# Output product by one level of Strassen: seven block products for eight, block sums on GpSimd

## The chip, the cores and the metric

One Trainium2 chip; the program runs on one of its cores. A core has five engines with queues of their own: TensorE (PE in the profile, its weight loads PEld), VectorE (DVE), ScalarE (ACT), GpSimd (POOL) and SyncE (SP), which here only starts DMAs. The engines run in parallel and meet at semaphores; each takes its own instructions in order. TensorE reads SBUF and writes PSUM; DVE and ACT read and write both; GpSimd reads and writes SBUF alone. The metric is the device time of one run in microseconds (us), the median of several.

## The reference

Two stages. Attention through a small memory, for 8 batches of 8 heads, 576 tokens, head width 64 and 32 memory slots; then a bilinear feed-forward over the 4608 tokens.

```python
a = softmax(phi, over tokens)                    # 576 x 32 per head
k_m, v_m = a.T @ k, a.T @ v                      # 32 x 64 each
x = softmax(q @ k_m.T / 8) @ v_m                 # 576 x 64 per head, 8 heads side by side: 512
h = (x @ w1) * (x @ w2)                          # 512 -> 1024, elementwise product
out = (h @ w3) @ w_out                           # 1024 -> 1024 -> 512
```

All inputs and the output are float32; the weights come in as float64.

## The kernel before, in words

Two products are folded ahead of the tokens. W = w3 w_out (1024 x 512) is built once on chip from converted weights ("C" steps convert a tile of float64 to float32 on DVE and ACT, "W" steps are its matmuls, "K" steps take it out of PSUM). For each batch M = v_m w1 and v_m w2 (per head, 256 memory rows against 2 x 1024 columns) is made in four quarters of 256 columns of h, so that x w1 and x w2 become products of the attention weights with M.

To get near float32 from the fast float32r matmul, each operand is split into a rounded high part and the rest (`split`, lines 114 to 116: ACT casts, another engine subtracts), and a product is three matmuls: high by high, high by low, low by high.

A batch passes through two stages on TensorE:

- The A stage: 16 units "A" (`ab_unit`), one for each of 8 row tiles of 128 columns of h and each half of 288 tokens. A unit is 12 matmuls of 128x128 weights against 288 columns: 6 into a PSUM bank "a" (x w1) and 6 into a bank "b" (x w2). ACT copies a to `a_sb` (line 458), DVE multiplies b by it into `gr` (line 460), and `gr`, which is G of `out = G W`, is split into `gh` and `gl` (line 463).
- The output stage: row tiles of 128 tokens. A tile is four steps "O" (`out_part`) of 6 matmuls: weights are 128 tokens of G, moving are the 512 columns of W. 24 matmuls add up in one bank "o"; ACT copies it to `osb`, and a DMA stores it. 576 is four and a half tiles, so odd batches do five tiles and even ones four; 36 in all.

Between these units stand the attention steps of the next batch and the one after, by name: `top` (maximum mx of phi on DVE, line 162), `exp` (ACT, line 168), `turn0` and `turn4` (transposes of phi on TensorE, line 184 and 188, copied by ACT), `mem` (memories, line 199), `blocks` (transposes, line 224, and four DVE copies to km and vm), `sc` (scores), `se`, `sn`, `pr` (softmax over the memories and the split into `ah` and `al`), and the M steps (line 298, then split into `mh` and `ml`).

PSUM has 8 banks: two each of "a", "b" and "o", and one pair "x". The pair x serves the transposes, `blocks`, half of the scores and some M steps; whoever comes next into x waits until the engine that reads it has finished. In the kernel before, M steps written "Mp" use banks a and b instead, "M" uses x, and all four for the next batch stand in the output stage.

The order on TensorE and on SyncE is the order of the program, which the strings START, FIRST, SECOND and STEADY write out by hand: FIRST is batch 0, SECOND batch 1, STEADY the rest; a name with "+" belongs to the batch after next. The order on DVE, ACT and GpSimd is set by a scheduler that moves instructions by a model of their times. `fetch` and `load` issue DMAs; a load goes out when its tile is free.

Of the kernel before, what the change touches and what calls it, by code (L numbers as in the profile page):

```python
# [35 lines left out]
mem+ sc0 sc1p Mp O kv3 se0 O se1 O q2 sn0 O pr0 O sn1 O pr1 M Mp Mp O O phi3 O O blocks+ O O O O O O Oo Oo Oo Oo  # L36
# [4 lines left out]
def memory_attention__then__bilinear_ffn_kernel(  # L41
# [22 lines left out]
    P = 128  # L64
# [7 lines left out]
    DO = w_out.shape[1] // 2  # L72
    HALF = S // 2
# [17 lines left out]
    half = NF // 2  # L91

    def w_half(r):

        return [const.tile([P, half, DO], F32R, name=f"W{x}{r}") if r == 0 else
                const.tile([P, half, DO], F32R, name=f"W{x}{r}", tag=f"wo{i}") for i, x in enumerate("hl")]

    Wh, Wl = [list(x) for x in zip(w_half(0), (None, None))]
# [56 lines left out]
    def attention(b):  # L155
# [129 lines left out]

    m_tags = (2, 3, 4, 0, 5, 6, 7, 1)

    def memory_weights(b):
# [3 lines left out]
        def step(q, banks):  # L292
# [12 lines left out]
            mh = const.tile([P, NT, 2, FQ], F32R, name=f"mh{q}", tag=f"m{m_tags[2 * q]}")  # L305
            ml = const.tile([P, NT, 2, FQ], F32R, name=f"ml{q}", tag=f"m{m_tags[2 * q + 1]}")
# [22 lines left out]
    raws, w3s = {}, {}  # L329
    free_m = [1, 2, 3, 4, 0, 5, 6, 7, 1]  # L330
    wos = [const.tile([P, half, DO], F32, name=f"wo{i}", tag=f"wo{i}") for i in range(2)]
# [18 lines left out]
    def convert(i):  # L350
# [3 lines left out]
        if kind == "w12":  # L354
            y = w12_sb[at[0]][:, at[1]]
        elif kind == "wo":
            y = wos[at // half][:, at % half : at % half + n]
        else:
            y = const.tile([P, n, CW // 2], F32, name="w3", tag=f"m{free_m.pop(0)}")
            for j in range(n):  # L360
                w3s[int(kind[2]), at + j] = y[:, j]
        if i < FIRST_LATE:
            u = init.tile([P, CW], I32, name="u", bufs=2)
        elif i % 2:
            u = att.tile([P, 5 * NT * P], I32, name="ua", tag="a")
        else:
            u = att.tile([P, 2, S], F32R, name="al", tag="al", bufs=2).rearrange("p t s -> p (t s)").bitcast(I32)
# [18 lines left out]
    def product(r, k):  # L386
# [3 lines left out]
        x = w3s.pop((r, k))  # L390
        for i in range(4):
            nc.tensor.matmul(  # L392
                pw[r][i],
                lhsT=x[:, i * P : (i + 1) * P],
                rhs=wos[k // half][:, k % half],
                start=k == 0,
                stop=k == NF - 1,
            )

    def keep(r, i):  # L400
        if r == 1 and Wh[1] is None:
            Wh[1], Wl[1] = w_half(1)
        split(Wh[r][:, i], Wl[r][:, i], pw[r][i])
# [8 lines left out]
    with tc.tile_pool(name="init", bufs=1) as init:  # L412
# [4 lines left out]
        for what in START:  # L417
# [4 lines left out]
            elif what[0] == "K":  # L422
                keep(int(what[1]), int(what[2]))
# [155 lines left out]
```

## Time and profile before

| | us |
|---|---|
| median of 3 runs | 551.91 (551.74 to 552.37) |
| span of the profiled execution | 548.7 |
| median beyond that span | 3.2 |
| TensorE busy | 531.0 |
| DVE, ACT, GpSimd busy | 306.7, 248.9, 14.0 |

The profile is of one execution. A row of a timeline gives start, duration, engine, line, operation, output and inputs, and in brackets the idle time before it with what ended it. A row of groups ends with busy time, mean of one in ns, and the engine's idle time before them. Matmuls are pipelined: the duration of one is longer than the distance to the next, so rates are read from starts.

### The profile page before, as it was taken

The numbers are of one execution on the slowest core, as the hardware profiler recorded it, in microseconds if no ns is written. First come the engines' busy times: TensorE is split into PE (matmuls) and PEld (weight loads), VectorE is DVE, ScalarE is ACT, GpSimd is POOL, SyncE is SP. The second block draws the span as 40 slices with busy tenths as digits, with TensorE's granted clock in tenths as the row PEclk, the third lists the DMA queues.
The fourth block names the chain that finished last, engine by engine and source line by source line (L and its number), as shares of the span: only waits on it lengthen the run. The fifth ranks groups of instructions, "written<-read, shape, count | busy, mean of one in ns | idle before, by whom it ended". The sixth has DMA issues, their size and how long they took to land.

```text
span 548.7 us, 9743 instructions
## 1 busy us (share of the span) xinstructions
PE 531.0 (97%) x4024; PEld 427.4 (78%) x4024; DVE 306.7 (56%) x584; ACT 248.9 (45%) x494; POOL 14.0 (3%) x22
## 2 busy tenths in 40 slices
PE   4799999999999999999999999999999999999997
PEld 1344357976998689968996899869986899689985
DVE  4877996357367715593458425673567045915400
ACT  5886966524454325452544335443544044514310
POOL 0000004400000000000000000000000000000000
PEclk9999999999999999999999999999999999999999
DMA  8999827036334510072008210351022100010011
GB/s 300 408 361 391 295 77 272 31 113 229 118 139 171 171 40 20 2 278 82 20 1 280 81 39 1 149 174 57 1 59 69 39 20 2 20 44 15 1 38 57
DMA packets 24987, 64.05 MB, mean 117 GB/s; under 512 B 1776, under 2 KB 2032, under 8 KB 24944
## 3 DMA queue, kind: packets, MB, share of 16 engines
q1 hardware_dynamic: 24944, 63.45, 32.6%
q8 instruction: 31, 0.51, 0.4%
q14 instruction: 12, 0.10, 0.1%
HBM read 54.00 MB, written 9.44 MB: 116 GB/s over the span
## 4 chain that ended last, share of the span: by engine, by line
PE 89%; DVE 6%; DMA 2%; issue 1%; ACT 1%; SPq 0%; DVEq 0%; ACTq 0%
PE o L473 37%; PE b L449 18%; PE a L449 18%; PE a L298 2%; PE a L392 2%; PE b L392 2%; DMA raw<-in_w3T 2%; PE o L199 2%; PE x L298 2%; DVE w L382 2%; PE x L184 1%; PE b L298 1%; PE x L199 1%; PE x L239 1%; DVE w L381 1%
## 5 line engine op out<-in xcount | busy, mean ns | idle before, releaser
L473 PE MATMUL o<-Wh,gh 128*128 128x512 f32 x288 | 115.4, 401 | 0.0
L473 PE MATMUL o<-Wl,gh 128*128 128x512 f32 x288 | 112.8, 391 | 0.0
L473 PE MATMUL o<-Wh,gl 128*128 128x512 f32 x288 | 112.5, 391 | 0.0
L460 DVE TENSOR_TENSOR gr<-b,a_sb 128x288 f32<-128x288 f32 x128 | 58.6, 458 | 94.0 <-PE b L449 87.0
L115 ACT CAST gh<-gr 128x288 fp32r<-128x288 f32 x128 | 55.4, 433 | 100.8 <-DVE gr L460 100.5
L116 DVE TENSOR_TENSOR gl<-gr,gh 128x288 fp32r<-128x288 f32 x112 | 51.2, 458 | 55.5 <-ACT gh L115 55.3
L449 PE MATMUL b<-ah,mh 128*128 128x288 f32 x256 | 76.0, 297 | 1.7 <-DVE gr L460 1.2
L449 PE MATMUL a<-ah,mh 128*128 128x288 f32 x256 | 77.3, 302 | 0.0
L449 PE MATMUL a<-al,mh 128*128 128x288 f32 x256 | 75.6, 295 | 0.1
L449 PE MATMUL b<-al,mh 128*128 128x288 f32 x256 | 75.5, 295 | 0.0
L449 PE MATMUL a<-ah,ml 128*128 128x288 f32 x256 | 75.3, 294 | 0.0
L449 PE MATMUL b<-ah,ml 128*128 128x288 f32 x256 | 75.3, 294 | 0.0
L473 PEld LDWEIGHTS o<-Wh,gh 128*128 128x128 f32 x288 | 54.1, 188 | 22.6 <-issue 11.9
L491 ACT COPY osb<-o 128x512 f32<-128x512 f32 x31 | 18.1, 585 | 100.5 <-PE o L473 87.7
L473 PEld LDWEIGHTS o<-Wl,gh 128*128 128x128 f32 x288 | 54.1, 188 | 12.4
L473 PEld LDWEIGHTS o<-Wh,gl 128*128 128x128 f32 x288 | 54.1, 188 | 10.9
L458 ACT COPY a_sb<-a 128x288 f32<-128x288 f32 x128 | 50.2, 394 | 3.3 <-PE a L449 3.3
L449 PEld LDWEIGHTS a<-ah,mh 128*128 128x128 f32 x256 | 48.0, 187 | 3.1 <-issue 1.0
L449 PEld LDWEIGHTS b<-ah,mh 128*128 128x128 f32 x256 | 48.0, 187 | 2.4 <-DVE gr L460 1.6
L449 PEld LDWEIGHTS a<-al,mh 128*128 128x128 f32 x256 | 48.1, 188 | 0.7 <-DVE al L116 0.3
L449 PEld LDWEIGHTS b<-ah,ml 128*128 128x128 f32 x256 | 48.2, 188 | 0.0
L449 PEld LDWEIGHTS a<-ah,ml 128*128 128x128 f32 x256 | 48.2, 188 | 0.0
(98 smaller groups left out, 663.1 us busy)
## 6 DMA issues: line engine op xcount, KB each, us to landing
kv<-in_kv SPq DMA_DIRECT2D x16, 1024.0 KB, 7.2
q<-in_qT SPq DMA_DIRECT2D x8, 1152.0 KB, 10.7
out<-osb SPq DMA_DIRECT2D x31, 256.0 KB, 2.0
raw<-in_w3T SPq DMA_DIRECT2D x7, 1024.0 KB, 11.9
ph<-in_phiT SPq DMA_DIRECT2D x8, 576.0 KB, 3.9
raw<-in_w SPq DMA_DIRECT2D x4, 1024.0 KB, 16.4
raw<-in_w_out SPq DMA_DIRECT2D x3, 1024.0 KB, 10.5
kv<-in_w SPq DMA_DIRECT2D x3, 1024.0 KB, 14.3
```

The source lines that it names most:

```text
L115: nc.scalar.copy(out=hi, in_=src)
L116: engine.tensor_tensor(out=lo, in0=src, in1=hi.bitcast(F32), op=ALU.subtract)
L184: nc.tensor.transpose(ps[:, c, t], v["ph"][:, t, at : at + P], ident)
L199: nc.tensor.matmul(ps[t][h * M : (h + 1) * M, : 2 * D], lhsT=v["a"][:, i, t, h * M : (h + 1) * M], rhs=kvt[i][:, (4 * t + h) * 2 * D : (4 ...
L298: nc.tensor.matmul(ps[t][g * M : (g + 1) * M], lhsT=vm[b % 2][d, g], rhs=w12_sb[q][d, :, g], start=True, stop=True,)
L382: nc.vector.tensor_tensor(out=y, in0=y, in1=u, op=ALU.add)
L392: nc.tensor.matmul(pw[r][i], lhsT=x[:, i * P : (i + 1) * P], rhs=wos[k // half][:, k % half], start=k == 0, stop=k == NF - 1,)
L449: nc.tensor.matmul(p, lhsT=x[:, t, w, fc : fc + P], rhs=y[:, n, t * HALF : (t + 1) * HALF], start=i == 0, stop=i == len(todo) - 1,)
L458: nc.scalar.copy(out=a_sb, in_=ps[0])
L460: nc.vector.tensor_tensor(out=gr, in0=ps[1], in1=a_sb, op=ALU.mult)
L473: nc.tensor.matmul(v["p"], lhsT=x[f][:, at : at + P], rhs=y[f // half][:, f % half], start=f == 0 and k == 0, stop=f == NF - 1 and k == 2,)
L491: nc.scalar.copy(out=osb, in_=v["p"])
```

## The change

G and W are each cut into 2 x 2 blocks, and `out` is computed with one level of Strassen's method (the variant with 4 sums on either side and shared sums on the output): seven products of blocks for eight. With tokens cut into halves n (288 tokens) and the inner dimension into alternating tiles k, G has blocks `r00, r01, r10, r11` (tile `raw`), one for each half and parity of the tile.

- The operands change places: weights are now blocks of W (128 columns at a time), moving are 288 tokens. The output is stored transposed, 512 x 4608, and turned on the host.
- `weight_sums` forms four differences of W's blocks on GpSimd, once for each half of W's rows; `weight_split` splits the seven block operands into `Th`, `Tl` (ACT casts, GpSimd subtracts for the first half, DVE for the second). `keep` is now a copy alone.
- `ab_unit` writes the product to `raw` (line 486); `add` forms four sums of G's blocks on GpSimd, in place (line 461); `operand` splits a block sum for one product into a slot `s0` to `s3`, subtracting on DVE, and for products 5 and 3 on GpSimd.
- `out_part` is one product j and one half t of 128 output columns: 12 matmuls of 288 columns. The order is 1, 2, 6, 7, 4, 5, 3. Products 1, 6, 7 and 4 add up in banks "o", with a copy of the bank to `ev` after 1, 6 and 7 (line 529); 2, 5 and 3 go to banks a and b, and DVE adds `ev` on the way out (line 541).
- The M tiles get two buffers by parity of the quarter. One M step for the next batch stays in the output stage, and three ("m") go into the batch's own A stage. All use pair x; "Mp" is gone.
- Scratch for the conversions moves to other tiles, `ah` and `al` have one buffer instead of two, and the scratch for software DMAs shrinks to make room.

```diff
 STEADY = """
-A top+ A exp+ A norm+ A A turn0+ A A turn4+ A A A A A A A A A
-mem+ sc0 sc1p Mp O kv3 se0 O se1 O q2 sn0 O pr0 O sn1 O pr1 M Mp Mp O O phi3 O O blocks+ O O O O O O Oo Oo Oo Oo
+A m A top+ A exp+ A A m norm+ A A turn0+ A A m A turn4+ A A A A A A
+mem+ sc0 sc1p O kv3 se0 O se1 O q2 sn0 O pr0 O sn1 O pr1 O M O phi3 O O blocks+ O O O O
...
-            mh = const.tile([P, NT, 2, FQ], F32R, name=f"mh{q}", tag=f"m{m_tags[2 * q]}")
-            ml = const.tile([P, NT, 2, FQ], F32R, name=f"ml{q}", tag=f"m{m_tags[2 * q + 1]}")
+            mh = const.tile([P, NT, 2, FQ], F32R, name=f"mh{q}", tag=f"mh{q % 2}")
+            ml = const.tile([P, NT, 2, FQ], F32R, name=f"ml{q}", tag=f"ml{q % 2}")
...
+    def weight_sums(r):
+        t = late.tile([P, 3, 2, DC], F32, name="sums", tag="ev")
+        b11, b12, b21, b22 = [block(r, k, j) for k in range(2) for j in range(2)]
+        sub = lambda out, x, y: nc.gpsimd.tensor_tensor(out=out, in0=x, in1=y, op=ALU.subtract)
+        sub(t[:, 2], b22, b12)
+        sub(b12, b12, b11)
+        sub(t[:, 1], b22, b12)
+        sub(t[:, 0], b21, t[:, 1])
+        sums[r] = {1: b11, 2: b21, 3: b22, 4: t[:, 0], 5: b12, 6: t[:, 1], 7: t[:, 2]}
...
+        split(Th[j][:, at], Tl[j][:, at], sums[r][j], nc.vector if r else nc.gpsimd)
...
+    HOME = {1: 0, 2: 1, 6: 2, 4: 3, 7: 0, 5: 1, 3: 2}
+
+    def operand(j, i, n=1):
+        if i == 0:
+            s = HOME[j]
+            slots[j] = (big if s < 2 else late).tile([P, 2, NP, TH], F32R, name=f"s{s}", tag=f"s{s}")
+        x = {1: raw[0][0], 2: raw[0][1], 4: raw[1][1], 6: raw[1][1], 7: raw[1][0], 5: raw[0][0], 3: raw[0][1]}[j]
+        h, l = slots[j][:, 0, i : i + n], slots[j][:, 1, i : i + n]
+        split(h, l, x[:, i : i + n], nc.gpsimd if j in (5, 3) else nc.vector)
...
-        nc.vector.tensor_tensor(out=gr, in0=ps[1], in1=a_sb, op=ALU.mult)
-        split(gh[f][:, at : at + HALF], gl[f][:, at : at + HALF], gr, nc.vector if b else nc.gpsimd)
+        i, k = divmod(f, 2)
+        nc.vector.tensor_tensor(out=raw[n][k][:, i], in0=ps[1], in1=a_sb, op=ALU.mult)
+        if (n, k) == (0, 1) and i % 2:
+            operand(1, i - 1, 2)
+            operand(2, i - 1, 2)
+        elif (n, k) == (1, 0):
+            add(a21, a11, a21, ALU.subtract)
+        elif (n, k) == (1, 1):
+            operand(4, i)
+            add(a22, a22, a21, ALU.subtract)
+            if i % 2:
+                operand(6, i - 1, 2)
+                j = slice(i - 1, i + 1)
+                add(raw[0][0][:, j], raw[0][0][:, j], raw[1][1][:, j], ALU.add)
+                add(raw[0][1][:, j], raw[0][1][:, j], raw[1][1][:, j], ALU.subtract)
+
+    ORDER = [(j, t) for j in (1, 2, 6, 7, 4, 5, 3) for t in range(2)]
...
-            for k, (x, y) in enumerate(((gh, Wh), (gl, Wh), (gh, Wl))):
+        for i in range(NP):
+            for k, (w, g) in enumerate(((Th, 0), (Th, 1), (Tl, 0))):
                 nc.tensor.matmul(
-                    v["p"],
-                    lhsT=x[f][:, at : at + P],
-                    rhs=y[f // half][:, f % half],
+                    p,
+                    lhsT=w[j][:, i, c],
+                    rhs=x[:, g, i],
...
+        if t == 1 and j in (1, 2, 6):
+            for i in range(0, NP, 2):
+                operand({1: 7, 2: 5, 6: 3}[j], i, 2)
...
+        if j in (1, 6, 7):
+            nc.scalar.copy(out=ev[:, (1, 6, 7).index(j), t], in_=p)
+            return
...
+        if j == 4:
+            nc.scalar.copy(out=osb[:, t], in_=p)
+        else:
+            nc.vector.tensor_tensor(out=osb[:, t], in0=p, in1=ev[:, {2: 0, 5: 2, 3: 1}[j], t], op=ALU.add)
```

Three places show how the queues change. The first is ACT in the A stage of batch 3, between the copy of turn0 (x to a, 1024 wide) and that of turn4 (x to a, 128 wide). Before:

```order
L185 COPY a_3300<-x_3341 128x1024
L458 COPY a_sb_3365<-a_3351 128x288
L115 CAST gh2_502<-gr_3367 128x288
L458 COPY a_sb_3385<-a_3371 128x288
L189 COPY a_3300<-x_3391 128x128
```

After:

```order
L181 COPY a_2904<-x_2946 128x1024
L484 COPY a_sb_2970<-a_2956 128x288
L111 CAST s3_2868<-r11_506 128x288
L484 COPY a_sb_2995<-a_2981 128x288
L111 CAST s2_2976<-r11_506 128x576
L111 CAST mh3_3007<-x_2998 128x1024
L484 COPY a_sb_3025<-a_3011 128x288
L185 COPY a_2904<-x_3028 128x128
```

Between the two users of x there now stands a third, the batch's last M step (mh3 from x), and one A unit (one a_sb) between it and turn4.

The second is DVE in the A stage of batch 1 around the fifth unit: `gr` and `r00` are the units' products, mx the maximum of phi for batch 3, km and vm the copies of `blocks`. Before:

```order
L116 TENSOR_TENSOR gl1_509<-gr_1307,gh1_501 128x288
L162 TENSOR_REDUCE mx_1471<-ph_1311 128x2
L227 TENSOR_SCALAR km0_77<-x_1384 64x128
L228 COPY vm0_79<-x_1384 64x128
L227 TENSOR_SCALAR km0_77<-x_1384 64x128
L228 COPY vm0_79<-x_1384 64x128
L173 TENSOR_SCALAR sm_1493<-sm_1493 128x2
L460 TENSOR_TENSOR gr_1373<-b_1364,a_sb_1371 128x288
```

After:

```order
L112 TENSOR_TENSOR s3_1389<-r11_506,s3_1389 128x288
L158 TENSOR_REDUCE mx_1549<-ph_1393 128x2
L169 TENSOR_SCALAR sm_1581<-sm_1581 128x2
L170 RECIPROCAL sm_1581<-sm_1581 128x2
L486 TENSOR_TENSOR r00_503<-b_1446,a_sb_1453 128x288
L112 TENSOR_TENSOR s0_1500<-r00_503,s0_1500 128x576
L112 TENSOR_TENSOR ml2_1466<-x_1456,mh2_1465 128x1024
L223 TENSOR_SCALAR km0_77<-x_1476 64x128
```

The copies of `blocks` now come after the fifth unit's product, its split and an M quarter (ml2) that sits in x too; `blocks` takes x right after that M step, with no unit between.

The third is DVE at the end of the product stage of batch 3, after the change: al ends the attention of batch 4, mx belongs to batch 5, and osb are the output additions of product 5 (banks a and b).

```order
L112 TENSOR_TENSOR al_3311<-at_3309,ah_3310 128x576
L112 TENSOR_TENSOR ml0_3377<-x_3367,mh0_3376 128x1024
L158 TENSOR_REDUCE mx_3535<-ph_3393 128x2
L223 TENSOR_SCALAR km1_78<-x_3423 64x128
L224 COPY vm1_80<-x_3423 64x128
L223 TENSOR_SCALAR km1_78<-x_3423 64x128
L224 COPY vm1_80<-x_3423 64x128
L541 TENSOR_TENSOR osb_3443<-a_3430,ev_3231 128x288
```

Before, nothing that TensorE waits for stood behind mx here; now the addition that frees product 5's bank does.

More of the change, by code (lines that the diff above doesn't have):

```diff
@@ L72, in memory_attention__then__bilinear_ffn_kernel @@
     DO = w_out.shape[1] // 2
+    TH = S // 2
     HALF = S // 2
@@ L90, in memory_attention__then__bilinear_ffn_kernel @@
     w12_sb = [const.tile([P, 2, NG, FQ], F32, name=f"w12_{q}") for q in range(NQ)]
[L91 to L98, printed above, removed]
+    NP = NF // 2
+    DC = DO // 2
+    late = ctx.enter_context(tc.tile_pool(name="late", bufs=1))
     def psum(pool, name):
@@ L328, in memory_attention__then__bilinear_ffn_kernel @@
     BUFS = 5
-    raws, w3s = {}, {}
-    free_m = [1, 2, 3, 4, 0, 5, 6, 7, 1]
-    wos = [const.tile([P, half, DO], F32, name=f"wo{i}", tag=f"wo{i}") for i in range(2)]
+    raws, parts_of = {}, {}
+    free_wt = iter(range(14))
     init = None
@@ L389, in product, with block, weight_split @@
             pw[r] = [psum(*x) for x in (tags * 2, ((ps_o, "o"),) * 2 + tags)[r]]
-        x = w3s.pop((r, k))
+        x = parts_of.pop((f"w3{r}", k))
+        y = parts_of["wo", k] if r == 0 else parts_of.pop(("wo", k))
         for i in range(4):
[L392 to L398, printed above, removed]
-    def keep(r, i):
-        if r == 1 and Wh[1] is None:
-            Wh[1], Wl[1] = w_half(1)
-        split(Wh[r][:, i], Wl[r][:, i], pw[r][i])
+            nc.tensor.matmul(pw[r][i], lhsT=x[:, i * P : (i + 1) * P], rhs=y, start=k == 0, stop=k == NF - 1)
+    W, sums, Th, Tl = {}, {}, {}, {}
+    def keep(r, i):
+        if r not in W:
+            W[r] = late.tile([P, NP, DO], F32, name=f"W{r}", tag=f"s{2 + r}")
+        nc.scalar.copy(out=W[r][:, i], in_=pw[r][i])
+    def block(r, k, j):
+        return W[r].rearrange("p (i k) (j c) -> p i k j c", k=2, j=2)[:, :, k, j]
+    def weight_sums(r):
[7 more added lines that the diff above has]
+        sums[r] = {1: b11, 2: b21, 3: b22, 4: t[:, 0], 5: b12, 6: t[:, 1], 7: t[:, 2]}
+    def weight_split(j, r):
+        if r == 0:
+            Th[j], Tl[j] = [const.tile([P, NP, DC], F32R, name=f"T{x}{j}", tag=f"wt{2 * j - 2 + i}") for i, x in enumerate("hl")]
+        at = slice(2 * r, 2 * r + 2)
+        split(Th[j][:, at], Tl[j][:, at], sums[r][j], nc.vector if r else nc.gpsimd)
     todo = iter(range(len(tasks)))
@@ L423, in memory_attention__then__bilinear_ffn_kernel @@
                 keep(int(what[1]), int(what[2]))
+            elif what[0] == "T":
+                weight_sums(int(what[1]))
             elif what == "N":
@@ L499, in memory_attention__then__bilinear_ffn_kernel @@
     for b in range(B):
         v = {}
-        ab = iter([(n, f) for f in range(NF) for n in range(2)])
-        if b == 0:
-            ab = iter([(n, 2 * q + f) for q in range(NQ) for n in range(2) for f in range(2)])
-        parts = iter([(i, part) for i in range((S + b % 2 * REST) // P) for part in range(4)])
+        ab = iter([(n, 2 * i + k) for i in range(NP) for n in range(2) for k in range(2)])
+        parts = iter(ORDER)
+        m_now = m0 if b == 0 else m1
         if b + 1 < B:
@@ L511, in memory_attention__then__bilinear_ffn_kernel @@
                 out_part(b, *next(parts), v)
-            elif what == "Oo":
-                if b % 2:
-                    out_part(b, *next(parts), v)
+            elif what == "m":
+                m_now.pop(0)()
             elif what == "C":
```

99 lines of the change are left out of this document (52 added, 47 removed).

## The prediction

> **What bounds the kernel now.** I read the page's first and fourth parts first: which engine fills the span, and which work the chain that ended last is made of.
>
> ```profile
> span 548.7 us, 9743 instructions
> PE 531.0 (97%) x4024; PEld 427.4 (78%) x4024; DVE 306.7 (56%) x584; ACT 248.9 (45%) x494; POOL 14.0 (3%) x22
> PE 89%; DVE 6%; DMA 2%; issue 1%; ACT 1%; SPq 0%; DVEq 0%; ACTq 0%
> ```
>
> TensorE is the bound: 97% busy, 89% of the chain. DVE and ACT have slack on the average and GpSimd is nearly empty. So columns removed from TensorE come off the time one for one, and so does every new gap on TensorE. The median of the runs, 551.9 us, is 3.2 above this execution's span of 548.7; I make the sum on the span and carry the 3.2 along.
>
> Next the timeline of TensorE in a steady batch, for the pitch of back-to-back matmuls: start of one to start of the next.
>
> ```profile
> 224.75 0.29 PE L449 MATMUL a<-ah,mh 128*128 128x288 f32 x1
> 230.62 0.29 PE L449 MATMUL b<-ah,ml 128*128 128x288 f32 x1
> 235.28 0.39 PE L473 MATMUL o<-Wh,gl 128*128 128x512 f32 x1
> 243.07 0.39 PE L473 MATMUL o<-Wl,gh 128*128 128x512 f32 x1
> ```
>
> Between the first pair lie 44 steps: 5.87/44 = 133.4 ns for 288 columns. Between the second lie 34: 7.79/34 = 229.1 ns for 512. One unit "A" (12 matmuls) is thus 1.60 us.
>
> **The gain.** Before, the output stage has 36 row tiles of 24 matmuls: 864 x 0.2291 = 197.9 us. After, each of 8 batches has 7 products x 2 halves x 12 = 168 matmuls of 288 columns, 1344 in all. Their form (128x128 fp32r weights, 288 moving columns, a weight load each) is exactly the A unit's, so its pitch is the price, loads included: 1344 x 0.1334 = 179.3. That is 18.6 less: 9.4% for an eighth of the columns, because the short matmul is dearer per column. All else on TensorE (A units, four M steps a batch, attention, the weight product) keeps its count.
>
> **What DVE, ACT and GpSimd get, and what hides it.**
>
> ```profile
> L460 DVE TENSOR_TENSOR gr<-b,a_sb 128x288 f32<-128x288 f32 x128 | 58.6, 458 | 94.0 <-PE b L449 87.0 <-PE x L188 3.7 <-ACT gh L115 1.6
> L458 ACT COPY a_sb<-a 128x288 f32<-128x288 f32 x128 | 50.2, 394 | 3.3 <-PE a L449 3.3
> L115 ACT CAST gh<-gr 128x288 fp32r<-128x288 f32 x128 | 55.4, 433 | 100.8 <-DVE gr L460 100.5
> L115 ACT CAST ah<-at 128x576 fp32r<-128x576 f32 x16 | 10.7, 673 | 13.0 <-DVE at L274 13.0
> L116 DVE TENSOR_TENSOR al<-at,ah 128x576 fp32r<-128x576 f32 x16 | 11.5, 753 | 0.6
> L116 POOL TENSOR_TENSOR gl<-gr,gh 128x288 fp32r<-128x288 f32 x16 | 13.3, 834 | 96.5 <-ACT gh L115 96.5
> ```
>
> A batch's splits become 12 casts of 576 at 673 ns and 4 of 288 at 433: 9.8 us of ACT for 6.9 before. On DVE 8 subtractions at 753 and 4 at 458 (7.9 for 7.3) and 6 output adds near 458 (2.7). GpSimd gets 8 operations of 288 (834 ns) and 8 of 576. The last have no row: bounds are 0.83 (all fixed cost) and 1.67 (all per element); I take 1.5, nearer the second since the work is per element. That is 19 us of GpSimd in a batch of some 57. DVE and ACT gain under 4 us each per batch at 56% and 45% use; all this lies beside TensorE, and costs only where a TensorE instruction comes to wait. Walking the new queues with these durations, the operands are in time: the last one made from the final A unit (sum on GpSimd, cast, subtraction) is ready some 3 us after it, and the two products ahead of it take 6.4. Handing bank o from product to product needs a 394 ns copy within a 1.6 us half product. Output DMAs are 4 a batch for 4 or 5, off the path; the tail keeps one evacuation and one store.
>
> **Where TensorE comes to wait: pair x.** M now goes through pair x only, three of its four steps inside the A stage, where the transposes of phi use x too. What an M step through x costs until x is free, in batch 0:
>
> ```profile
> 95.80 1.09 PE L298 MATMUL x<-w,vm 64*32 64x512 f32 x16
> 96.82 0.40 PE L449 MATMUL a<-ah,mh 128*128 128x288 f32 x1
> 96.99 1.02 ACT L115 CAST mh<-x 128x1024 fp32r<-128x1024 f32 x1
> 98.05 1.23 DVE L116 TENSOR_TENSOR ml<-x,mh 128x1024 fp32r<-128x1024 f32 x1 [1.58 <-ACT mh L115]
> ```
>
> M ends at 96.82, x is free at 99.28: 2.46 us. In batches 2 to 5 one A unit stands between the fourth M step and turn4, in batch 1 one between the second and turn0. One unit covers 1.60, so TensorE stands 0.86 each time: 5 x 0.86 = **4.3 us**. Behind the waiting transpose all of TensorE waits. Without the unit as cover it would be 2.46.
>
> In batch 1 `blocks` follows its M step with no unit between: 2.46 at least. DVE's new order makes it longer: the maximum mx for batch 3 stands ahead of the fifth unit's product, and waits for a transfer issued only when turn4 has read phi.
>
> ```profile
> 144.89 0.39 SPq L123 DMA_DIRECT2D ph<-in_phiT  x1
> 148.81 1.35 DVE L162 TENSOR_REDUCE mx<-ph 128x2 f32<-128x1152 f32 x1 [0.85 <-DMA ph<-in_phiT]
> 86.82 0.78 ACT L168 ACTIVATE ph<-ph,mx 128x576 f32<-128x576 f32 x1 [0.57 <-DVE mx L162]
> 88.26 0.19 ACT L168 ACTIVATION_READ_ACCUMULATOR ph<-ph,mx 128x1 f32 x1
> 230.84 1.96 PE L199 MATMUL o<-kv,a 128*32 128x128 f32 x64
> 232.97 0.69 PE L239 MATMUL x<-q,km 64*32 64x288 f32 x16
> ```
>
> From issue to mx 3.92, mx 1.35, the two exponentials 1.63 (86.82 to 88.45). Counted from turn4's end: mx ends 5.3, exponentials 7.0, a_sb 7.4, the product 7.9, its cast 8.6, mh 9.6, ml and x free 10.9. TensorE gets there at 1.60 + 2.13 (memories, 230.84 to 232.97) + 1.60 + 1.02 = 6.35. Stall **4.5 us**; bounds 2.46 (mx not in the way) and 6.
>
> **The same mx behind the products.** In the product stage mx for the batch after next stands ahead of the output add of product 5, whose bank product 3 needs. In batch 0 the scores come three halves into the products. The chain from scores to the last al took 12.4 us in the quoted steady batch:
>
> ```profile
> 243.92 1.43 DVE L116 TENSOR_TENSOR al<-at,ah 128x576 fp32r<-128x576 f32 x2
> ```
>
> (232.97 to 245.35). Scores at 7.2 after the first product begins, al at 19 to 20.7 (the new rows interleave), phi in 3.9 later, mx and the add by 24.7 to 26.4; product 3 wants the bank at 23.6. Stall 1.1 to 2.8; I take **1.5**. In batches 1 to 5 the scores start first, the add is done at about 22.5 and the bank is wanted at 23.6: hidden by 1.1, which is what a phi later by that much would cost each time.
>
> **The start.** Before the A units DVE is the late one, and TensorE waits for it:
>
> ```profile
> 77.89 0.65 DVE L116 TENSOR_TENSOR Wl<-a,Wh 128x512 fp32r<-128x512 f32 x1
> 80.71 0.69 ACT L458 COPY a_sb<-a 128x288 f32<-128x288 f32 x2
> 83.19 0.40 PE L449 MATMUL b<-ah,mh 128*128 128x288 f32 x1 [0.58 <-DVE gr L460]
> 88.20 0.45 DVE L460 TENSOR_TENSOR gr<-b,a_sb 128x288 f32<-128x288 f32 x1
> L115 ACT CAST Wh<-a 128x512 fp32r<-128x512 f32 x3 | 1.8, 586 | 0.9 <-PE a L392 0.9
> ```
>
> Up to the fourth unit's product (88.20 before) DVE now has 7 Tl subtractions for 4 Wl, 3 x 0.6 = 1.8 more, and one of the conversions' adds (1.22) less: +0.6. ACT has 14 new casts of 586 ns. About one of them comes into the conversions' way (0.6), and three stand right ahead of the first a_sb: 1.8 later, of which DVE's own delay covers a part; I count 0.8. Together **+2.0**; bounds -1 (the casts fall in ACT's gaps) and +5 (ACT held by casts that wait for GpSimd's sums, four sums of 512 at 0.83 to 1.5 behind two splits).
>
> **Sum.** -18.6 + 4.3 + 4.5 + 1.5 + 2.0 = -6.3, so span 542.4, and 545.6 for the median: **546 us**.
>
> **GpSimd and DVE together.** One stretch of batch 0 shows both at work:
>
> ```profile
> 83.05 1.22 DVE L382 CUSTOM_DVE_ANT_0 w<-w,ua 128x2048 uint16<-128x2048 uint16 x1
> 83.68 1.25 POOL L116 TENSOR_TENSOR gl<-gr,gh 128x288 fp32r<-128x288 f32 x1 [82.38 <-ACT gh L115]
> 93.81 0.81 POOL L116 TENSOR_TENSOR gl<-gr,gh 128x288 fp32r<-128x288 f32 x1 [0.23 <-ACT gh L115]
> ```
>
> Beside DVE's two-input add GpSimd took 1.25 for 0.81; DVE kept its 1.22. So I let GpSimd stretch and DVE not. A DVE operation that starts while GpSimd already runs is not in the trace: bounds nothing, and a wait of a whole GpSimd operation, 0.83 to 1.5.
>
> The Trainium skill, "GPSIMD Engine Reference", section 4.1, says to keep two-input elementwise work on VectorE, and section 8 that both share SBUF interfaces and contend when DVE has two SBUF inputs: a rule against this change. The stretched 0.81 agrees with the sharing; who yields in the other order no run here shows.
>
> **Rivals.**
> 1. *DVE waits for GpSimd* (slower). If a two-input DVE operation stands until the running GpSimd one ends, the sixth operand's subtraction waits for two sums ahead, ml follows 1.7 later, and the 5 waits on x grow by 1.7: 8.5. Four attention operations per product stage lose about 1 each, so mx is 4 later: 4 in batch 0 and 2.9 past the 1.1 of cover in batches 1 to 5, 18.5. Together 27: 573. It decides from about 0.4 us more per two-input DVE operation, where these two eat the 6.3 and the cover. Against it: DVE's 1.22. Chance 0.10.
> 2. *phi later than 3.9 us, or the chain to al slower than walked.* 2.5 us later costs 1.4 in each of batches 1 to 5 and 2.5 in batch 0: 9.5, thus 555. For it: so many small rows on thin cover. Chance 0.15, a third of it past 553.
> 3. *The waits do not appear*: x freed in time, mx not in the way; only the start's +2.0 stays. 551.9 - 18.6 + 2.0 = 535.3. Against: the 2.46 is measured and TensorE's order is fixed. Chance 0.13.
> 4. *No change*: waits of 18.6 by chance. Chance 0.06.
>
> **How the numbers follow.** The forecast holds 0.56, with a range of its own of 541 to 551. Below 536 lies half of rival 3, above 557 rival 1 and a little: the range is 536 to 557. A measurement of this kernel can tell about 0.2%, 1.1 us. Faster by more: 0.54 of the forecast, 0.13 of rival 3 and 0.10 of rival 2: 0.77. Slower: rival 1 and 0.05 of rival 2: 0.15. Same: rival 4 and the forecast's other 0.02, 0.08.
>
> **What would show it.** Right: 133 ns pitch in the product matmuls; a gap of 0.8 to 1 before turn4 in batches 2 to 5, released by ml on DVE; one of 4 to 5 before `blocks` in batch 1; GpSimd's 576 at 1.4 to 1.6 with single ones stretched; DVE's subtractions still at 753. Wrong: a pitch over 140 ns, waits for bank o in the products, or DVE rows longer where GpSimd runs.

## The result and the profile after

The changed kernel takes 583.9 us (median of 4 runs, 583.4 to 586.7); the kernel before, on the same chip, 551.8. The ratio is 1.060, 95% interval [1.057, 1.063]: 32 us slower, where 6 us less were forecast. The first, second and fourth part of the page of the changed kernel:

```profile
span 582.3 us, 10894 instructions
PE 528.6 (91%) x4504; PEld 448.7 (77%) x4504; DVE 370.7 (64%) x593; ACT 278.7 (48%) x515; POOL 183.5 (32%) x149
PEclk9999897999899999999999999999999999989999
PE 53%; DVE 28%; DMA 7%; ACT 6%; issue 3%; POOL 1%; DVEq 0%; POOLq 0%
```

TensorE is still the busiest engine, but the chain that ended last now runs through DVE for 28% of the span (6% before). TensorE waits, and these are its waits (engine, line, tile, what it waited for; then total us, times, longest):

```profile
PE o L514 <- ACT ev L529: 10.3, 7, 2.1
PE a L386 <- DVE wt L375: 9.7, 2, 8.8
PE b L475 <- DVE r L486: 6.9, 1, 6.9
PE x L184 <- DVE ml L112: 5.5, 4, 1.4
PE a L514 <- DVE osb L541: 5.3, 5, 2.1
PE x L292 <- DVE w L375: 4.4, 1, 4.4
PE x L220 <- DVE ml L112: 3.9, 1, 3.9
```

The second row is the start, nearly as before (9.7 for 10.7). The fourth, and one transpose of 0.65 beside it, are the forecast's waits on pair x; the seventh is its wait before `blocks`. The others were not in the sum, or not at that size. Together TensorE stands idle for 50.5 us (sum of all gaps in its timeline) where it was 14.2.

The groups of DVE, then of GpSimd, with shapes kept apart:

```profile
L112 DVE TENSOR_TENSOR s<-r,s 128x576 fp32r<-128x576 f32 x64 | 60.3, 947 | 33.8 <-ACT s L111 33.8
L486 DVE TENSOR_TENSOR r<-b,a_sb 128x288 f32<-128x288 f32 x128 | 58.0, 454 | 68.5 <-PE b L475 63.5 <-PE x L184 4.5 <-ACT a_sb L484 0.5
L261 DVE TENSOR_TENSOR s_sb<-s_sb,ss 128x576 f32<-128x576 f32 x16 | 21.5, 1346 | 0.2
L112 DVE TENSOR_TENSOR al<-at,ah 128x576 fp32r<-128x576 f32 x16 | 17.5, 1091 | 4.1 <-ACT ah L111 3.8
L251 DVE TENSOR_REDUCE st<-s_sb 128x18 f32<-128x576 f32 x16 | 11.8, 745 | 0.2
...
L461 POOL TENSOR_TENSOR r<-r,r 128x288 f32<-128x288 f32 x64 | 57.8, 903 | 269.9 <-DVE r L486 212.9 <-DVE s L112 55.0 <-DVE sm L170 2.0
L461 POOL TENSOR_TENSOR r<-r,r 128x576 f32<-128x576 f32 x32 | 52.7, 1668 | 1.3
L112 POOL TENSOR_TENSOR s<-r,s 128x576 fp32r<-128x576 f32 x32 | 47.5, 1506 | 49.8 <-ACT s L111 49.8
```

Before, the multiplication of the third row (now line 261) had this row:

```profile
L265 DVE TENSOR_TENSOR s_sb<-s_sb,ss 128x576 f32<-128x576 f32 x16 | 11.4, 749 | 0.0
```

It takes 1346 ns now, the subtraction for al 1091 for 753, and the new splits of the same width 947. The operations have kept their form; what is new is the work on GpSimd beside them. Of the 16 multiplications the 10 that some GpSimd operation overlaps take 1698 ns on the mean, the other 6 take 758; of the 16 for al the 11 overlapped take 1248 and the other 5 take 745. The product of b and a_sb, with one input in PSUM, and the reduction keep their time. In the timeline of the product stage of batch 3 one sees how:

```profile
327.91 2.82 POOL L112 TENSOR_TENSOR s<-r,s 128x576 fp32r<-128x576 f32 x2 [5.09 <-ACT s L111]
329.43 1.91 DVE L261 TENSOR_TENSOR s_sb<-s_sb,ss 128x576 f32<-128x576 f32 x1
331.38 0.78 DVE L270 STREAM_TRANSPOSE at<-s_sb 128x576 f32<-128x576 f32 x1
332.19 0.67 ACT L111 CAST ah<-at 128x576 fp32r<-128x576 f32 x1 [3.10 <-DVE at L270]
332.77 1.24 ACT L111 CAST s<-r 128x576 fp32r<-128x576 f32 x2
333.92 0.69 ACT L529 COPY ev<-o 128x288 f32<-128x288 f32 x2
334.36 0.54 PE L514 MATMUL o<-s,Th 128*128 128x288 f32 x2 [1.51 <-ACT ev L529]
333.51 2.92 POOL L112 TENSOR_TENSOR s<-r,s 128x576 fp32r<-128x576 f32 x2 [2.78 <-ACT s L111]
335.21 1.84 DVE L112 TENSOR_TENSOR al<-at,ah 128x576 fp32r<-128x576 f32 x1 [0.75 <-ACT ah L111]
```

GpSimd's two splits end at 330.73; DVE's multiplication, begun at 329.43, ends 0.61 later, at 331.34. The second pair ends at 336.43, and al, begun at 335.21, ends 0.62 later. So DVE's row is a stand until GpSimd ends, and then most of its usual work. The rest is queues: `at` late on DVE, `ah` late on ACT, behind it in ACT's order two casts, behind these the copies of bank o that product 6 needs. TensorE stands 1.51 us, in each of batches 1 to 5.

The start is the other place. DVE, GpSimd and TensorE in the first units of batch 0, and the granted clock (after the four engines' and the weight loads' busy time) in the stretch behind it:

```profile
84.46 5.11 DVE L112 TENSOR_TENSOR Tl<-W,Th 128x512 fp32r<-128x512 f32 x3
83.90 1.75 POOL L403 TENSOR_TENSOR sums<-W 128x512 f32<-128x512 f32 x1
89.10 1.61 POOL L403 TENSOR_TENSOR sums<-W,sums 128x512 f32<-128x512 f32 x1
93.47 0.44 DVE L486 TENSOR_TENSOR r<-b,a_sb 128x288 f32<-128x288 f32 x1
93.97 0.61 PE L475 MATMUL b<-ah,mh 128*128 128x288 f32 x1 [6.91 <-DVE r L486]
94.38 0.44 PE L475 MATMUL b<-al,mh 128*128 128x288 f32 x1
94.62 0.44 PE L475 MATMUL b<-ah,ml 128*128 128x288 f32 x1
...
90.30:97.00 6.70, 3.03 (x12) 3.03 (x13) 6.70 (x9) 2.31 (x5) 0.41 (x1) 0.51 0.50 168
```

Four block sums of W run back to back on GpSimd from 83.90 to 90.71; three subtractions of W on DVE take 5.11 beside them, where one that stands alone (at 96.66) takes 0.67. The first product of a unit that stands behind them begins at 93.47, and TensorE has stood 6.91 us. Then it runs at half clock: matmuls 0.24 us apart (94.38 to 94.62) for 0.133.

### The profile page after: what moved, and what is told of

It reads as the page before. It is cut to its first block, busy times and chain, and to the rows that moved or that the text cites. A ratio compares the mean times of both kernels' runs of the same rounds, so it can differ in the third digit from the quotient of the medians.

```text
span 582.3 us, 10894 instructions
## 1 busy us (share of the span) xinstructions
PE 528.6 (91%) x4504; PEld 448.7 (77%) x4504; DVE 370.7 (64%) x593; ACT 278.7 (48%) x515; POOL 183.5 (32%) x149
## 4 chain that ended last, share of the span: by engine, by line
PE 53%; DVE 28%; DMA 7%; ACT 6%; issue 3%; POOL 1%; DVEq 0%; POOLq 0%
PE a L475 16%; PE b L475 16%; PE o L514 5%; DVE s L112 4%; DMA ph<-in_phiT 4%; PE a L514 4%; PE b L514 3%; PE x L292 3%; ACT s L111 3%; DVE s_sb L261 3%; DVE s_sb L244 2%; DVE st L251 2%; DVE s_sb L252 2%; PE a L386 2%; DVE ss L258 2%
## 5 line engine op out<-in xcount | busy, mean ns | idle before, releaser
L461 POOL TENSOR_TENSOR r<-r,r 128x288 f32<-128x288 f32 (+1 forms) x96 | 110.5, 1158 | 271.2 <-DVE r L486 212.9
L514 PE MATMUL o<-s,Th 128*128 128x288 f32 x512 | 105.5, 301 | 11.7 <-ACT ev L529 10.3
L111 ACT CAST s<-r 128x576 fp32r<-128x576 f32 (+1 forms) x128 | 76.0, 612 | 74.1 <-DVE r L486 45.4
L112 DVE TENSOR_TENSOR s<-r,s 128x576 fp32r<-128x576 f32 (+1 forms) x96 | 75.0, 784 | 49.3 <-ACT s L111 49.3
L486 DVE TENSOR_TENSOR r<-b,a_sb 128x288 f32<-128x288 f32 x128 | 58.0, 454 | 68.5 <-PE b L475 63.5
L514 PEld LDWEIGHTS o<-s,Th 128*128 128x128 f32 x512 | 82.9, 191 | 21.9 <-ACT ev L529 16.4
L514 PE MATMUL o<-s,Tl 128*128 128x288 f32 x256 | 76.3, 298 | 0.0
L112 POOL TENSOR_TENSOR s<-r,s 128x576 fp32r<-128x576 f32 x32 | 47.5, 1506 | 49.8 <-ACT s L111 49.8
L475 PEld LDWEIGHTS b<-al,mh 128*128 128x128 f32 x256 | 48.9, 191 | 0.0
L514 PEld LDWEIGHTS o<-s,Tl 128*128 128x128 f32 x256 | 48.9, 191 | 0.0
## 6 DMA issues: line engine op xcount, KB each, us to landing
kv<-in_w SPq DMA_DIRECT2D x3, 1024.0 KB, 14.5
```

The source lines that it names most:

```text
L111: nc.scalar.copy(out=hi, in_=src)
L112: engine.tensor_tensor(out=lo, in0=src, in1=hi.bitcast(F32), op=ALU.subtract)
L461: nc.gpsimd.tensor_tensor(out=out, in0=x, in1=y, op=op)
L475: nc.tensor.matmul(p, lhsT=x[:, t, w, fc : fc + P], rhs=y[:, n, t * HALF : (t + 1) * HALF], start=i == 0, stop=i == len(todo) - 1,)
L486: nc.vector.tensor_tensor(out=raw[n][k][:, i], in0=ps[1], in1=a_sb, op=ALU.mult)
L514: nc.tensor.matmul(p, lhsT=w[j][:, i, c], rhs=x[:, g, i], start=first and i == 0 and k == 0, stop=i == NP - 1 and k == 2, skip_group_check ...
```

## The experiments

The ratios are to the kernel before on the chip of the same run, where its median lay between 550.5 and 552.4 us; so a difference of two medians from different chips can be off by some 2 us.

**What shares what.** A kernel that computes nothing of the reference and runs chains of DVE operations, alone and beside GpSimd.

```diff
+    stages = [(d, None, 4, 0) for d in D] + [(None, g, 0, 4) for g in G]
+    stages += [(d, "g576", 5, 5) for d in D]
```

> This kernel computes nothing of the reference: it only runs chains of VectorE operations, first alone, then beside a chain of GpSimd subtractions that read two SBUF tensors (576 and 288 wide) or one. Theory 1, exclusion: an operation of VectorE with two SBUF inputs and one of GpSimd never run at the same time; whichever starts later stands until the other has ended. Then a 576-wide VectorE subtraction that takes about 0.75 us alone takes 1.4 to 2.2 us on the mean beside 576-wide GpSimd subtractions (1.4 us alone), and the GpSimd ones stretch too; the broadcast form behaves alike; operations with a PSUM input (0.45), reductions (0.75) and stream transposes (0.78) keep their time; the uint16 form with one input took 1.74 for 0.75 once in the changed kernel, so one-input forms of this kind are held too. Rival, shared bandwidth: every form stretches by much the same factor, a transpose and a reduction as well, and by less than a whole GpSimd operation. Rival, no effect: all forms keep their time, and the long rows of the changed kernel come from something else.

Its timeline: four DVE subtractions (two inputs in SBUF) alone, four one-input operations alone, four GpSimd subtractions alone; then five and five together for the subtraction, for a product with a PSUM input, for the reduction, and for the one-input operation.

```profile
7.76 3.13 DVE L42 TENSOR_TENSOR d_tt<-x,y 128x576 f32<-128x576 f32 x4
27.03 1.94 DVE L48 TENSOR_SCALAR d_ts<-x 128x576 f32<-128x576 f32 x4
34.22 5.82 POOL L53 TENSOR_TENSOR g<-gx,gy 128x576 f32<-128x576 f32 x4
46.49 8.94 POOL L53 TENSOR_TENSOR g<-gx,gy 128x576 f32<-128x576 f32 x5
47.83 8.22 DVE L42 TENSOR_TENSOR d_tt<-x,y 128x576 f32<-128x576 f32 x5
65.97 2.41 DVE L44 TENSOR_TENSOR d_ps<-b,y 128x288 f32<-128x288 f32 x5
83.18 3.89 DVE L46 TENSOR_REDUCE d_red<-x 128x18 f32<-128x576 f32 x5
97.95 6.72 DVE L48 TENSOR_SCALAR d_ts<-x 128x576 f32<-128x576 f32 x5
```

A subtraction takes 0.78 alone and 1.64 beside GpSimd; GpSimd's goes from 1.46 to 1.79. A pair costs 1.79 for a sum of 2.24, so they take turns, with some 0.45 of one overlapping the other. The one-input operation goes from 0.49 to 1.34, more than doubled though it has one input. The product from PSUM (0.48) and the reduction (0.78) are what they are alone (1.92/4 and 3.11/4), the stream transpose too (0.80 for both). Beside one-input copies on GpSimd (0.71 alone) DVE is held too: the subtraction takes 1.06 and the one-input operation 0.76. Shared bandwidth is out: three of nine forms do not change at all. The Trainium skill, "SBUF — State Buffer", section "Who interferes with whom", says just this: operations with two SBUF inputs and one-input operations in a two-port mode exclude GpSimd, reductions never do, and issue order decides who stands. The runs agree with these clauses; the prediction drew on another page, which names the contention and not its rule.

**GpSimd without reading.** Every sum and split on GpSimd becomes a fill with zeros of the same tile, once, and in a second kernel three times in a row. Both kernels leave GpSimd's sums and low parts out of the computation.

```diff
-        nc.gpsimd.tensor_tensor(out=out, in0=x, in1=y, op=op)
+        nc.gpsimd.memset(out, 0.0)
```

> Each GpSimd operation (block sums and splits) is replaced by a GpSimd fill with zeros of the same tile, which reads nothing: the sums and the low parts that GpSimd makes are left out of the computation, the order on TensorE stays. Theory 1: without reads by GpSimd VectorE's two-input rows are at 0.75 us and 1.22, and the time falls by what the holding cost: 11.9 us up to and in batch 0, 2.7 in each of batches 1 to 5, 0.55 at four transposes, 3 in the other batches: 30.7, thus 553 us (548 to 560). Rival, order alone: 578 to 584. Were a fill to hold VectorE as well, its rows would stay long wherever a fill runs.

> As in the run with fills, GpSimd's sums and low parts are left out of the computation, but each operation is now three fills in a row, so that GpSimd is about as long on each tile as with its subtractions (3 x 0.34 = 1.0 us for 0.83 to 0.91 on 288 columns, 3 x 0.58 = 1.7 for 1.51 to 1.67 on 576). Theory 1, exclusion by reading: the fills read nothing and hold nobody, so VectorE's two-input rows stay at 0.75 and the time stays near the 554.5 of single fills: 553 to 560. Rival, GpSimd is too slow as a producer: the 28 us between 583.9 and 554.5 came from operands that GpSimd delivers late, so three fills bring them back: 575 to 584 with VectorE's rows still at 0.75.

Measured: 554.5 us with single fills (ratio 1.006 [1.004, 1.009]) and 558.2 with three (1.012 [1.008, 1.017]). The groups of the kernel with three:

```profile
L116 DVE TENSOR_TENSOR s<-r,s 128x576 fp32r<-128x576 f32 x64 | 47.6, 754 | 28.3 <-ACT s L111 28.3
L116 DVE TENSOR_TENSOR al<-at,ah 128x576 fp32r<-128x576 f32 x16 | 12.1, 754 | 3.6 <-ACT ah L111 2.7
...
L466 POOL MEMSET r<- 128x288 f32 x192 | 65.2, 339 | 213.9 <-DVE r L491 181.2 <-DVE s L116 26.7
L466 POOL MEMSET r<- 128x576 f32 x96 | 55.8, 581 | 29.3 <-DVE s L116 27.1
```

GpSimd is as long on each tile as in the changed kernel (3 x 339 and 3 x 581 ns for 903 and 1668), busy 193 us for 184, and DVE's rows are at 754. Of the 32 us lost, 25.8 (583.9 - 558.2) go with the reading, and 3 to 4 more with GpSimd's slowness as a producer (558.2 - 554.5; by the two ratios 3.2). In the batches the fills run beside the same DVE work: 14 of the 16 subtractions for al and 15 of the 16 multiplications overlap a fill, and take 756 and 740 ns. So what goes there is the exclusion, and it is the larger part. But a fill also waits for no input: the sums of W that begin at 83.90 in the changed kernel are filled from 70.05 on, so at the start the 25.8 hold earlier sums as well as the exclusion, and this run does not part the two. The wait before the last transpose of phi has both causes: it is 0.65 with single fills, 1.24 with three, 1.39 in the changed kernel. There ml stands behind the split of operand 6, whose sum comes late from GpSimd; with three fills lateness alone makes the 1.24, and in the changed kernel, where the sum is a little earlier, the split takes 1.39 for 0.75 beside GpSimd (at 366.44, in batch 4's A stage).

**The work on VectorE instead.** All of it, or the splits of products 5 and 3 alone.

```diff
-        split(h, l, x[:, i : i + n], nc.gpsimd if j in (5, 3) else nc.vector)
+        split(h, l, x[:, i : i + n])
...
-        nc.gpsimd.tensor_tensor(out=out, in0=x, in1=y, op=op)
+        nc.vector.tensor_tensor(out=out, in0=x, in1=y, op=op)
```

> All sums and splits that GpSimd does in the changed kernel go to VectorE; GpSimd does nothing in the batches. Theory 1 (GpSimd holds VectorE): VectorE's 576-wide subtraction is back at 0.75 us (0.95 on the mean in the changed kernel), the broadcast multiply at 0.75 (1.35), the conversions' add at 1.22; VectorE's busy time is 371 less some 36 of holding plus some 86 of moved work, 421 us, and still the time falls, to 563 us (555 to 575), since the waits that the holding caused go: the 8.6 us gap in the first units of batch 0, the 1.5 us waits on the evacuations. Rival, order alone: the waits come from the order of TensorE and from long queues, and more work on VectorE makes them longer: 584 to 600 us. Rival, the M steps alone: about 1.35 us of every batch is lost by the M steps standing singly; that part (11 us in all) stays in either case.

> Only the splits of the operands of products 5 and 3 go from GpSimd to VectorE; the block sums and the start stay on GpSimd. Theory 1: in the product stage nothing holds VectorE any longer, so the broadcast multiply (1.35 us) and the second attention subtraction (1.09) come back to 0.75, the 1.5 us wait of product 6 on ACT's evacuation shrinks under 0.5 and the 0.9 us wait of product 3 on VectorE's output add goes: some 2 us in each of batches 1 to 5, about 10 in all, 574 us (570 to 578). The 1.4 us before the last transpose of phi stays, and the start stays. Rival, order alone: four subtractions of 0.75 more in VectorE's queue per batch, waits as long or longer: 584 to 592.

Measured: 568.1 us with all of it (1.031 [1.028, 1.034]), 577.5 with the splits alone (1.048 [1.045, 1.050]). DVE does 143 operations more and still the time falls by 16. The waits of TensorE with all work on DVE:

```profile
PE x L184 <- DVE ml L112: 5.9, 4, 1.5
PE a L514 <- DVE osb L541: 4.6, 4, 1.3
PE o L514 <- ACT ev L529: 3.4, 6, 1.1
PE b L475 <- DVE r L486: 3.0, 3, 2.5
```

The waits on the evacuation fall from 10.3 to 3.4 (4.8 with the splits alone). Of the waits on the output adds the one of batch 0, 2.07, goes, but those of batches 1 to 4 grow, from 3.2 in all to 4.6 (4.0 with the splits alone, where I expected them to go). There the maximum of phi still stands ahead of the add, and waits for its transfer, which goes out when the last al has ended (205.30 and 205.33 in batch 1); DVE itself is idle for 1.58 ahead of it. TensorE, held at product 6 for 0.48 instead of 1.51, comes to product 3 sooner: 4.5 after that transfer's start, where it was 5.7. These waits are part of the miss, 568 and 577.5 for 563 and 574. In the first units of batch 0 waits of 2.6 and 2.6 and 6.8 us at a granted clock of 0.50 stay too with all work on DVE.

**The waits on pair x.** Only the order on TensorE is changed.

```diff
-A m A top+ A exp+ A A m norm+ A A turn0+ A A m A turn4+ A A A A A A
+A m A top+ A exp+ A A m norm+ A A turn0+ A A m A A turn4+ A A A A A
```

(In batch 1 likewise, and `blocks` moves ahead of its M step.)

> The changed kernel with another order on TensorE and nothing else: a second unit stands between an M step and the transpose of phi that follows it (batches 1 to 5), and in batch 1 the transposes of the memories come one unit after them and ahead of the M step. Theory 1 (exclusion is the larger part, the waits on pair x a smaller one that comes on top): the gaps of 1.4 us before the last transpose of phi in batches 2 to 5 (5.6), of 0.65 and 3.9 in batch 1 (4.5) go, nothing else moves, 583.9 - 10.1 = 574 us (571 to 577). Rival: the time is set by the GpSimd-VectorE-ACT chain, and TensorE meets the same waits later in the batch: 581 to 585.

Measured: 570.5 us (1.033 [1.030, 1.036]), 13.4 less than the changed kernel. The waits on x by `turn0`, `turn4` and `blocks` are gone; only a 0.38 stays in batch 1. That is 9.7 us. The time at half clock falls from 20.5 to 17.1 us in all, which is another 1.7; what the remaining 2 us are stays open. The forecast's waits on pair x were thus real, avoidable by the place of the transposes and of `blocks`, and some 10 us of the 583.9.

**Both, and phi later.**

```diff
-... O M O phi3 O O blocks+ O O O O
+... O M O O O blocks+ O O O phi3 O
```

> All of GpSimd's work on VectorE, the order of TensorE as in the run with a second unit between M and the transposes, and phi of the batch after next is loaded three product halves later, so that its maximum stands behind the output adds on VectorE. Theory 1: 568.1 measured with all work on VectorE, less four gaps of 1.45 before transposes, 4.6 in batch 1, and the waits on the output adds in batches 1 to 4 (1.32, 1.26, 1.22, 0.79): 15.0, thus 553 us (549 to 557). Rival, VectorE is the bound now at 72%: the waits move to other places, 560 to 568.

> GpSimd keeps only the block sums of the batches; the splits of products 5 and 3 and the whole weight work of the start are on VectorE; order and load of phi as in the run before it in this list. Theory 1: 577.5 measured with the splits alone moved; the start's holding goes (batch 0's products began at 121.6 there and at 116.0 with all work on VectorE: 5.6), and the order's 5.6 + 4.5 + the output adds' 4.1: 557.7 us (553 to 561). If holding in the A stage, which stays here (block sums beside the splits of products 1, 2, 4 and 6), reaches TensorE, this is slower than the run with all work on VectorE by more than 3 us; if not, the two are alike.

Measured: 555.9 us with everything on DVE (1.007 [1.005, 1.010]) and 561.1 with the batches' block sums left on GpSimd (1.016 [1.013, 1.018]). The first expectation was 553; of the waits on transposes only 0.4 us is left, and those on output adds are gone; new ones of 0.3 to 1.15 stand around the fourth unit of batches 2 to 5, since the later maximum and its exponentials are now ahead of the first units' product and copy. Leaving the sums on GpSimd costs 5 us, more than the 3 that I had set as the mark, but not where I expected it: TensorE's waits on the units are alike (4.7 and 4.6 for 4.6 and 4.5), and what grows are the waits in the products, on the evacuation (4.8 for 3.5) and behind the memories (1.3 for none). Whether exclusion, late sums or another order in the queues does that, these two runs do not tell. 555.9 is the fastest form of the changed kernel that leaves nothing out, and still slower than the kernel before.

**Single M steps.** In the kernel before, the three M steps in a row are set apart.

```diff
-... pr1 M Mp Mp O O phi3 O O blocks+ ...
+... pr1 M O Mp O phi3 Mp O O blocks+ ...
```

> The kernel before with one thing changed: the three M steps that stand together in the product stage of batches 1 to 6 stand singly, with a row tile between. Theory: each switch from one kind of matmul to an M step and back costs 0.09 + 0.11 us, so two more pairs of switches cost 0.4 us a batch and a single M step 0.1 more than one in a row: 0.4 to 0.8 in each of 6 batches, 2.4 to 4.8 us in all, 0.4% to 0.9%. Rival: the M steps' position is free, no difference above 0.2%.

Measured: 556.4 us (1.007 [1.005, 1.009]), 4.1 more. Batches 1 to 6, from the first unit of batch 1 to that of batch 7, of the kernel before and of this one; columns are length, busy time with instructions of TensorE, weight loads, DVE, ACT and GpSimd, then the granted clock:

```profile
138.94:491.90 352.96, 352.96 (x2923) 302.80 (x2922) 192.74 (x393) 146.13 (x329) 0.00 (x0) 1.00 0.23 80
...
140.85:498.13 357.28, 357.28 (x2923) 300.32 (x2922) 193.32 (x393) 147.03 (x329) 0.00 (x0) 1.00 0.23 80
```

The same instructions, no idle time, the same clock, and 4.3 us more: 0.72 a batch, 0.36 for each M step that leaves its neighbours. It shows in the starts: from the last product matmul ahead to the first behind, three M steps in a row take 3.06 us (243.07 to 246.13 in the kernel before), a single one 1.33 (245.61 to 246.94 here), and the first matmul behind is followed by the next after 0.34 for a pitch of 0.23. The changed kernel has four single M steps a batch for one and a row of three, so it pays this too, about 5 us over its batches (an estimate from this run: 0.72 x 7). Its single M steps cost the same: 1.24 from 224.48 to 225.72, which is 1.11 beyond the pitch of 0.13, as 1.33 is 1.10 beyond 0.23. The fourth, which stood right behind the scores before, is not in the estimate.

**Later weight splits.** To mend batch 0 of the form with everything on DVE, the splits of W's blocks are queued behind the unit that precedes them; in the second kernel phi also comes in the A stage.

```diff
-        split(Th[j][:, at], Tl[j][:, at], sums[r][j], nc.vector if r else nc.gpsimd)
+        with tc.issue_after(last["a_sb"]), tc.issue_after(last["r"]):
+            split(Th[j][:, at], Tl[j][:, at], sums[r][j])
```

> All of GpSimd's work on VectorE with the new order on TensorE and the later phi (555.9 measured), and the splits of the weight blocks queued on ACT and VectorE behind the copy and the product of the unit that precedes them in the program. Theory: the gaps of 2.6 and 2.9 us at the third unit of batch 0 and the half clock behind them (27 matmuls at 0.24 for 0.133 us, 3 us) go, 5 to 8 us: 549 us (547 to 552), at or under the kernel before. Rival: VectorE has no room left in batch 0 and the weight splits delay the operand splits before the products: 553 to 557.

> As the run with late weight splits, and phi of the batch after next is loaded in the A stage behind the first unit, so that its maximum (1.35 us on VectorE) doesn't stand ahead of the second unit's product, where the two runs with the later phi had gaps of 0.3 to 1.15 and 0.28 us in each of batches 2 to 5. Theory: some 0.8 us in each of 4 batches less than the run with late weight splits: 3 us. Rival: the maximum stands in the way wherever it is put in the A stage; no difference.

Measured: 560.6 us (1.014 [1.010, 1.017]) and 559.8 (1.013 [1.011, 1.016]): slower than 555.9, as the rival said, and beyond its 553 to 557. Of the waits of the first:

```profile
PE o L515 <- DVE s L112: 4.4, 2, 3.5
PE o L515 <- ACT s L111: 2.6, 1, 2.6
```

They stand in the first products of batch 0, which wait for operands that DVE has not split yet. The gaps of the first units have moved there, and longer time at half clock has come with them (17.1 us for 6.8 in the form that took 555.9). Between these two kernels 0.8 us, within their spread: the waits behind the maximum stay, 0.8 to 1.1 in each of batches 2 to 5, in another place.

**The bare arithmetic.** Fills on GpSimd, the new order, and phi later.

> The kernel with single fills on GpSimd (its sums and low parts are left out of the computation) and, on top, the order of TensorE with a second unit between M and the transposes and the later phi: the method's arithmetic on TensorE without the exclusion and without most waits on pair x. Theory: 554.5 measured with fills, less the transposes' waits (4 x 0.65 in batches 2 to 5, 0.66 + 3.87 in batch 1) = 7.1, thus 547 us (545 to 550); what then is left of the 15 to 18 us that the products save is about 5, since single M steps (0.35 each by the run on the kernel before, 2 a batch), batch 0 and the half clock take the rest. Rival: the waits come back elsewhere and it stays at 552 to 555.

Measured: 550.7 us (0.999 [0.997, 1.001], 10 runs), no difference from the kernel before; expected were 547. The profiled execution had a granted clock of 0.999 and 547.9; most others had 0.987 to 0.993 and some 550.7. So even with the sums for nothing, no exclusion and no long waits on x, the saving on the products is used up. The profiled executions of both kernels, at a clock of 0.999 and 1.000, show by what. From each TensorE start to the next, waits left out, the products take 181.4 us for 200.9, but the units 214.5 for 208.1, the M steps 32.6 for 30.2 and the scores 9.1 for 8.1, though their counts are the same; and the waits are 21.5 for 14.2. That is 19.5 saved, 9.8 lost beside single M steps and other breaks in the rows of matmuls, and 7.3 in waits; some 2.5 of the span are left, and the lower clock of most executions takes these.

## Why the prediction was wrong

The sum again, on the spans (548.7 to 582.3, +33.6; forecast -6.3). Waits are read from TensorE's timeline. The row on M steps is the estimate above; half clock is half of TensorE's busy time in the five stretches with a granted clock of 0.51 to 0.53 (2.8, 3.0, 3.4, 3.4 and 3.3 us); the rest is by subtraction. In it are the first matmuls behind gaps, which take 0.24 us for 0.13, and the fourth M step of a batch.

| term | forecast | measured |
|---|---|---|
| products | -18.6 | -20.3 |
| transposes of phi behind M | +4.3 | +6.2 |
| `blocks` behind M in batch 1 | +4.5 | +3.9 |
| product 3 behind the maximum, batch 0 | +1.5 | +2.1 |
| the same, batches 1 to 4 | 0 | +3.2 |
| product 6 behind the evacuation | 0 | +10.3 |
| first product behind the memories | 0 | +1.3 |
| start and first units | +2.0 | +9.3 |
| M steps standing singly | 0 | about +5 |
| half clock | 0 | about +8 |
| rest | 0 | +4.6 |

- **The gain** was right. Between these rows of the product stage lie 33 matmuls:

```profile
327.17 0.30 PE L514 MATMUL o<-s,Tl 128*128 128x288 f32 x1
331.53 0.29 PE L514 MATMUL o<-s,Tl 128*128 128x288 f32 x1
```

  4.36/33 = 132 ns, for 133.4 forecast; 1344 of them are 177.6 us for 197.9.
- **The waits on x** were right in place and number, and 10.1 us for 8.8 together. For `blocks` the chain was as walked. Behind M the wait was 1.39 for 0.86 in batches 2 to 5, since ml stands behind a split as well, and 0.65 in batch 1.
- **"So I let GpSimd stretch and DVE not"** is the step that failed. It rested on one pair of rows in which DVE had started first, and on reading GpSimd's 1.25 as a stretch. That row ends at 84.93, 0.66 after DVE's at 84.27: it is GpSimd that stands until DVE ends. The other order was in the trace too, though with a one-input operation; it begins inside GpSimd's 83.68 to 84.93 and takes 1.02 where this line's mean is 0.75:

```profile
84.54 1.02 DVE L377 TENSOR_SCALAR ua<-kv 128x1024 uint16<-128x1024 uint16 x1
```

  The order is what decides: whoever starts second stands. DVE's two-input rows grew, and with them every thin cover of the forecast: "hidden by 1.1" became 0.5 to 1.0 of waiting, the evacuation that I walked as free came 1.5 late, and the start left its bounds (9.3 for -1 to +5) as GpSimd's work on W held the weight splits and conversions. 25.8 of the 32 us go when GpSimd stops reading; at the start some of that is earlier sums.
- **Rival 1** had the mechanism, at a chance of 0.10. Its price of 27 beyond the forecast is near the 25.8 by luck, since its places were half right: the attention in the product stage, yes; but the waits on x that were to grow by 1.7 each grew by 0.5, the waits on the add were 3.2 in batches 1 to 4 for its 14.5, and it missed the start and ACT's evacuations, which stand two queues behind. Its 573 is 11 short of the 583.9.
- **"All else on TensorE ... keeps its count"** was true and not enough. The count stays, the neighbours do not: an M step alone costs 0.36 more than one in a row, and in the bare form units, M steps and scores together lose 9.8 of the 19.5 that the products save; waits take most of what is left.
- **The clock** was taken as full. The sum priced each gap by its length; a long one, or several close together, can cost again in half clock.
- The gain itself was thin: 18.6 us is 3.4% of the time, spread over 8 batches as 2.3 each, against a dozen small additions to three engines. I priced the ones that the order showed, and let the chance of a wait between engines stand at 0.10.

## What to carry to other kernels

Before moving elementwise work to GpSimd, list the DVE operations that run at that time. By the runs here those with two SBUF inputs, and the one-input `TENSOR_SCALAR` and copy, take turns with a GpSimd operation that reads SBUF, at nearly the length of the whole GpSimd operation; those that read one input from PSUM, reduce or transpose do not. A pair of rows that shows one order of starts says nothing of the other; measure both before taking a price from it. And price a step that moves by what stands beside it in its new place, not by its own duration.

## What the runs showed of the hardware that was not expected

- A DVE `TENSOR_SCALAR` or copy with one fp32 or uint16 SBUF input is held as long as a two-input one: 0.49 us alone, 1.34 beside 576-wide GpSimd subtractions.
- GpSimd's fill does not hold DVE's two-input operations: the subtraction stayed at 754 ns beside 193 us of fills.
- Half clock (granted clock 0.50) comes in stretches of 3.4 us or a multiple, 3.4 and 6.8 in the changed kernel, up to 13.7 in others. In the changed kernel all five waits of 2.07 us or more behind the first matmuls were met by one, and none of the waits of 1.66 or less. But the length of a single wait does not decide: one of 3.04 in the kernel before (up to 19.55) was followed by full clock, and so was one of 2.13 in the kernel with the new order alone; and in the kernel with phi in the A stage half clock ran from 82.88 to 86.29 behind waits of only 0.94 and 0.54. The Trainium skill, "TensorE: Matmul & The Clock Gate", section "Why this matters for your kernels", sets the mark at gaps of about 3 us; here half clock came behind shorter ones, and no run here gives a length that is safe.
- An M step (matmuls of 64x32 tiles) between others costs TensorE time without a wait in any view: 0.36 us more for one taken out of its row, all of it inside "busy". That it is the change of the kind of matmul as such is the likely reading; no run changes the kind alone.
